# The end of a streaming attention kernel: one store instead of two, and a last weight load cut in two

## The chip, the cores and the metric

The kernel runs on one core of one Trainium2 chip. The metric is the device time of one execution in microseconds, and each kernel was executed several times. The profiled span, from the first to the last instruction of the program, is about 2.1 us shorter than that time: 1321.6 us of span belong to 1323.67 us of time. Times of one kernel scatter by some tenths of a microsecond.

## The reference, cut to what matters

Two decode-attention blocks, A and B, each process a single query row with 32 heads. Their output rows lie side by side.

```python
# A: 32 heads, 32768 cached keys and values of 128 numbers each, one query row of 512 numbers
q = (x @ wq) per head                          # wq: 512 x 4096
p = softmax(q k^T / sqrt(128));  o = p v
a = concat_heads(o) @ wo                       # wo: 4096 x 512 -> one row of 512
# B: the same with 8 shared key/value heads and only the last 4096 keys
out = concatenate([a, b], axis=-1)             # 1 x 1 x 1024, bf16
```

## The kernel before

Almost all the work is streaming the 32 heads of A's caches. This document is about what comes after them: the output projection of A, whose weights `wo` are the last thing that the kernel loads. On the chip `wo` is a tile of 128 partitions, and each partition holds 32 chunks of 512 numbers (1 KB per chunk and partition). Chunk `a` is multiplied by column `a` of the attention output `oz`. The weights come in five loads, cut at these chunks:

```python
WO_CUTS = {"A": (0, 11, 19, 25, 29, 32), "B": (0, 16, 32)}
```

The first eleven chunks accumulate into one full row. All later ones run as pairs: the left and the right half of the row (256 columns each) run side by side on two parts of the matmul array, into rows 0 and 64 of one bank. In the last three pairs of the kernel before, the two halves start 3 to 4 ns apart and the pairs 108 to 109 ns.

```python
def halves(self, e, bank, lhsT, rhs, begin, end, only=(0, 1)):
    for i in only:
        inst = e.matmul(bank[64 * i:64 * i + 1, 0:256], lhsT=lhsT, rhs=rhs[:, 256 * i:256 * i + 256], ...,
                        tile_position=(0, 64 * i))

def store(self, bank, i, dep):
    row = slice(64 * i, 64 * i + 1)
    out, src = self.out_sb[row, :], bank[row, 0:256]
    if i == 0:
        o = self.op("dve", lambda v: v.tensor_copy(out, src), dep)
    else:
        o = self.op("act", lambda e: e.activation(out=out, in_=src, func=ACTF.Copy), dep)
    self.op("act" if i else "sp", lambda e: e.dma_start(self.out[0, :, 256 * i:256 * i + 256], out).then_inc(
        self.outsem[f"A{i}"], 16), o)

def emit_proj(self):
    # ... B's 32 chunks; a copy of their four strips (DVE); `rows`: one f32 matmul that adds them; B's store ...
    # ... chunks 0 to 10 of A into one row; a copy of that row (DVE) ...
    # ... chunks 11 to 30 in pairs, each part waiting for its load; ahead of chunk 25 the row of chunks 0 to 10 is added in ...
    for i in range(2):
        o = self.op("pe", lambda e, i=i: self.halves(e, self.PT, oz[:, 31:32], wo[:, 512 * 31:512 * 32], False, True, (i,)),
                    (self.wosem["A"][-1], 16), self.c["A"]["ozop"])
        self.store(self.PT, i, o)
```

Each half therefore has its own copy engine (the vector engine, DVE, or the scalar engine, ACT), its own store and its own completion semaphore, a counter on which an engine can wait. At the very end the sync engine (SP) waits for the three stores in the order B, A0, A1.

## Time and profile before

| | kernel before |
|---|---|
| time, first 3 runs | 1323.66, 1323.75, 1323.96 us |
| profiled span | 1321.6 us |
| read from HBM | 570.43 MB, 432 GB/s over the span |
| granted TensorE clock | 0.836 of full speed |
| last weights' semaphore full | 1318.848 us |
| end of span minus that | 2.737 us |

The moment at which a load's semaphore is full is called its landing. In the views, PE is the matmul array and PEld its weight loads. Times of single events to a nanosecond, such as the last two rows, come from the semaphore records of the trace, since the views of the profile don't print them. The instruction records show how the sync engine takes its three final waits, in two instructions: a separate event-semaphore instruction (1321.127) waits for A0 and A1, and the branch behind it (1321.204), 77 ns later, carries the wait for B. One view: the chain of work that ended last (start, length, what). These are a few of its pieces from the value matmuls of the last head on:

```profile
1301.34 5.88 PE psACC L656 x64
...
1312.20 0.70 DVE pb L740
1312.91 0.04 issue
1312.95 1.02 PE psACC L741 x2
1313.97 2.27 PE psT L745 x11
1316.24 3.15 PE psPT L719 x42
1319.39 0.02 issue
1319.42 0.41 DVE out_sb L727
```

It names the matmul array, between its stages the vector engine (seven pieces, 2.66 us, of which one is shown), and no load.

### The profile page before, as it was taken

To read this page: it belongs to the slowest core of one execution; us is meant where nothing else is said; L and a number is where in the kernel's file an instruction comes from. 1 tells how busy PE (TensorE), PEld (TensorE's weight loads), DVE (VectorE), ACT (ScalarE), POOL (GpSimd) and SP (SyncE) were. 2 spreads that over 40 slices of the span, in tenths; PEclk is the share of its full clock that TensorE was granted. 3 is DMA by queue.
4 is the path that set the end of the run, shared out by engine and by line. 5 is a ranking of instruction groups with operands and counts; after the bars stand their busy time and mean duration, and the time that the engine had idled before them with its cause. 6 is when DMAs were issued, how large, how long until landed. Compare 5 with 4: busy or idle time off the path is not lost. (4 is left out here: it accounts for less than half of the span.)

```text
span 1321.6 us, 28783 instructions
## 1 busy us (share of the span) xinstructions
PE 969.7 (73%) x13243; PEld 676.6 (51%) x13243; DVE 751.8 (57%) x1341; ACT 55.2 (4%) x168; POOL 2.6 (0%) x22
## 2 busy tenths in 40 slices
PE   4675768777677878776787777678777667877787
PEld 3353446555444655544465544445554445555453
DVE  3563556664555666455566645556665456665564
ACT  0000000000000000000000000000000000000000
POOL 0000000000000000000000000000000000000000
PEclk9886788887878888788888878888887788888788
DMA  9999999999999999999999999999999999999998
GB/s 402 435 436 429 440 432 430 440 434 432 435 434 434 432 436 438 428 436 436 428 438 434 428 438 434 428 440 432 431 440 432 434 434 432 436 432 434 440 428 365
DMA packets 13217, 570.59 MB, mean 432 GB/s; under 512 B 1555, under 2 KB 1558, under 8 KB 1942
## 3 DMA queue, kind: packets, MB, share of 16 engines
q1 hardware_dynamic: 12916, 570.43, 99.8%
q8 instruction: 8, 0.13, 0.0%
q10 hardware_dynamic: 290, 0.00, 0.0%
q14 instruction: 3, 0.02, 0.0%
HBM read 570.43 MB, written 0.00 MB: 432 GB/s over the span
## 5 line engine op out<-in xcount | busy, mean ns | idle before, releaser
L557 DVE COPY kt<-psT 128x1024 bf16<-128x1024 bf16 x1056 | 655.3, 684 | 235.9 <-PE psT L553 234.3
L553 PE MATMUL psT<-ident,kbuf 128*128 128x128 bf16 x8448 | 580.3, 234 | 166.6 <-DMA kbuf<-in_A_k_cache_dram 152.5
L553 PEld LDWEIGHTS psT<-ident,kbuf 128*128 128x128 bf16 x8448 | 540.7, 106 | 258.8 <-DMA kbuf<-in_A_k_cache_dram 160.5
L656 PE MATMUL psACC<-vbuf,ptsb 128*4 128x512 bf16 (+1 forms) x2112 | 187.4, 532 | 22.8 <-ACT ptsb L631 22.0
L576 PE MATMUL psS<-kt,qw 128*32 128x512 bf16 x2048 | 157.7, 385 | 14.8 <-DVE kt L557 14.8
L670 DVE TENSOR_SCALAR oc_A<-psACC,hot_A 128x128 f32<-128x128 f32 x32 | 11.2, 351 | 252.1 <-PE psG L683 252.1
L656 PEld LDWEIGHTS psACC<-vbuf,ptsb 128*4 128x4 bf16 (+1 forms) x2112 | 60.5, 111 | 140.1 <-issue 93.1
L604 ACT ACTIVATE psb<-psS,nb_A 128x512 bf16<-128x512 f32 x32 | 22.0, 687 | 1167.4 <-DVE nb_A L603 1167.4
L576 PEld LDWEIGHTS psS<-kt,qw 128*32 128x32 bf16 x2048 | 34.1, 95 | 57.3 <-DVE kt L557 30.4
L683 PE MATMUL psG<-oc_A,hw 128*32 128x128 f32 (+1 forms) x128 | 19.3, 227 | 52.3 <-DVE oc_A L672 52.3
L683 PEld LDWEIGHTS psG<-oc_A,hw 128*32 128x32 f32 x128 | 11.4, 109 | 62.4 <-DVE oc_A L672 55.0
L628 PE MATMUL psPT<-ident,psb 128*128 128x128 bf16 x136 | 18.2, 278 | 34.0 <-ACT psb L604 34.0
L672 DVE SCALAR_TENSOR_TENSOR oc_A<-psACC,hot_A,oc_A 128x128 f32<-128x128 f32 x96 | 33.7, 351 | 3.4
L593 DVE TENSOR_REDUCE tr_in<-psS 128x1 f32<-128x512 f32 x34 | 23.5, 692 | 17.2 <-PE psS L576 17.2
L628 PEld LDWEIGHTS psPT<-ident,psb 128*128 128x128 bf16 x136 | 10.3, 119 | 37.1 <-ACT psb L604 36.7
L597 PE MATMUL psACC<-rows,tr_in 128*1 128x64 f32 x64 | 8.7, 218 | 25.6 <-DVE tr_in L593 25.6
L631 ACT ACTIVATE ptsb<-psPT 128x512 bf16<-128x512 bf16 x34 | 20.3, 597 | 30.7 <-PE psPT L628 30.7
L597 PEld LDWEIGHTS psACC<-rows,tr_in 128*1 128x1 f32 x64 | 2.7, 81 | 35.1 <-DVE tr_in L593 35.1
L601 PE MATMUL psACC<-mr_A,nscale 1*128 1x1 f32 x64 | 12.1, 256 | 9.8 <-DVE mr_A L600 9.8
L601 PEld LDWEIGHTS psACC<-mr_A,nscale 1*128 1x128 f32 x64 | 9.4, 182 | 15.7 <-DVE mr_A L600 15.7
L495 PE MATMUL psACC<-vbuf,x_B 128*2 128x512 bf16 x32 | 3.6, 625 | 13.7 <-DMA x_B<-in_B_x_dram 13.7
L603 DVE COPY nb_A<-psACC 128x1 f32<-128x1 f32 x32 | 5.0, 158 | 15.0 <-PE psACC L601 15.0
(82 smaller groups left out, 76.5 us busy)
## 6 DMA issues: line engine op xcount, KB each, us to landing
kbuf<-in_A_k_cache_dram SPq DMA_DIRECT2D x4, 4096.0 KB, 23.1
kbuf<-in_B_k_cache_dram SPq DMA_DIRECT2D x2, 4096.0 KB, 31.9
vbuf<-in_B_v_cache_dram SPq DMA_DIRECT2D x2, 4096.0 KB, 25.2
vbuf<-in_B_wq_dram SPq DMA_DIRECT2D x1, 4096.0 KB, 12.7
vbuf<-in_A_wq_dram SPq DMA_DIRECT2D x1, 4096.0 KB, 32.3
kbuf<-in_B_wo_dram SPq DMA_DIRECT2D x2, 2048.0 KB, 33.0
kbuf<-in_A_wo_dram SPq DMA_DIRECT2D x1, 1408.0 KB, 26.1
kbuf<-in_A_wo_dram SPq DMA_DIRECT2D x1, 1024.0 KB, 28.2
```

Of the source, the lines that this page charges most:

```text
L553: inst = e.transpose(T[:, 128 * k:128 * k + 128], src[:, DH * k:DH * k + DH], self.ident[:, :])
L557: self.copies.append(self.op("dve", lambda v: v.tensor_copy(KT[:, :], T[:, :]), o, to="pe"))
L576: inst = e.matmul(self.S[32 * c:32 * c + 32, :], lhsT=win, rhs=self.kt[(bb + c // 2) % NKT][:, 512 * (c % 2):512 * (c % 2) + 512], start=b ...
L593: o = dve(lambda v: v.reduce_max(tr["in"][:, 0:1], self.S[:, :], axis=AXX), self.sdone, self.k_pool, to="pe" if name == "A" else None)
L597: o = self.op("pe", lambda e: e.matmul(self.ACC[0:1, 0:64], lhsT=tr["in"][:, 0:1], rhs=self.rows64[:, :], start=True, stop=True, skip_grou ...
L601: o = self.op("pe", lambda e: e.matmul(self.ACC[:, 64:65], lhsT=self.nscale[:, :], rhs=t["mr"][0:1, :], start=True, stop=True, skip_group_ ...
L604: self.sread = self.op("act", lambda s: s.activation(out=self.psb[:, :], in_=self.S[:, :], func=ACTF.Exp, bias=t["nb"][:, k:k + 1], scale= ...
L628: inst = e.transpose(PT[:, 128 * jj:128 * jj + 128], self.psb[:, 128 * jj:128 * jj + 128], self.ident[:, :])
L631: self.ptread = self.op("act", lambda s: s.activation(out=self.ptsb[:, :], in_=PT[:, 0:512], func=ACTF.Copy), self.psread, to="pe")
L656: inst = e.matmul(acc[32 * c:32 * c + rows, 0:512], lhsT=lhsT, rhs=rhs, start=begin, stop=end, tile_position=(0, 32 * c), skip_group_check ...
L672: o = self.op("dve", lambda v, src=src, hot=hot: v.scalar_tensor_tensor(out=oc, in0=src, scalar=hot, in1=oc, op0=ALU.mult, op1=ALU.add), p ...
L683: return self.op("pe", lambda e: e.matmul(self.G[0:32, c0 + c:c0 + c2], lhsT=win, rhs=t["oc"][g % len(t["oc"])][:, c:c2], start=False, sto ...
```

## The change

Two ideas for the last three microseconds. First, the last load of three chunks becomes one of two and one of a single chunk, so that less work is left when the last bytes arrive. Second, both halves are copied into one row of 512 numbers on one partition, and a single store by the sync engine takes it out.

```diff
-        self.out_sb = sb("out_sb", [128, 256], BF16)
+        self.out_sb = sb("out_sb", [1, 512], BF16)
...
-        self.outsem = {n: s(f"outsem_{n}") for n in ("B", "A0", "A1")}
+        self.outsem = {n: s(f"outsem_{n}") for n in self.X}
...
-    WO_CUTS = {"A": (0, 11, 19, 25, 29, 32), "B": (0, 16, 32)}
+    WO_CUTS = {"A": (0, 11, 19, 25, 29, 31, 32), "B": (0, 16, 32)}
...
     def store(self, bank, i, dep):
-        row = slice(64 * i, 64 * i + 1)
-        out, src = self.out_sb[row, :], bank[row, 0:256]
+        out, src = self.out_sb[0:1, 256 * i:256 * i + 256], bank[64 * i:64 * i + 1, 0:256]
         if i == 0:
-            o = self.op("dve", lambda v: v.tensor_copy(out, src), dep)
-        else:
-            o = self.op("act", lambda e: e.activation(out=out, in_=src, func=ACTF.Copy), dep)
-        self.op("act" if i else "sp", ... one store for each half ...)
+            return self.op("dve", lambda v: v.tensor_copy(out, src), dep)
+        return self.op("act", lambda e: e.activation(out=out, in_=src, func=ACTF.Copy), dep)
...
-            self.store(self.PT, i, o)
+            done.append(self.store(self.PT, i, o))
+        self.op("sp", lambda e: e.dma_start(self.out[0, :, 0:512], self.out_sb[:, :]).then_inc(self.outsem["A"], 16), *done)
```

## The prediction

> **What bounds the kernel now.** I read the page from the top. Transfers come first, in the slices of the span and in the queue table:

> ```profile
> DMA  9999999999999999999999999999999999999998
> ...
> q1 hardware_dynamic: 12916, 570.43, 99.8%
> HBM read 570.43 MB, written 0.00 MB: 432 GB/s over the span
> ```

> The 16 DMA engines are 90% busy or more in every slice but the last, and one load queue fills 99.8% of them. The kernel streams 570 MB at 432 GB/s, and nothing in the change alters a byte of that stream. So about 1318 of the 1321.6 us cannot move. What can move is what comes after the last weights have landed, so I asked for the timeline of the last 3.3 us (start, length, engine, line, [idle before <- who ended it]):

> ```profile
> 1317.80 0.59 PE L719 MATMUL psPT<-pb,e 1*1 1x256 f32 x4
> 1318.33 0.31 PEld L719 LDWEIGHTS psPT<-kbuf,oz_A 128*1 128x1 bf16 x8 [0.44 <-DMA kbuf<-in_A_wo_dram]
> 1318.33 1.06 PE L719 MATMUL psPT<-kbuf,oz_A 128*1 128x256 bf16 x14
> 1318.89 0.20 PEld L719 LDWEIGHTS psPT<-kbuf,oz_A 128*1 128x1 bf16 x6 [0.26 <-DMA kbuf<-in_A_wo_dram]
> 1319.42 0.41 DVE L727 CAST out_sb<-psPT 1x256 bf16<-1x256 f32 x1 [2.36 <-PE psPT L719]
> 1319.45 0.38 ACT L729 ACTIVATE out_sb<-psPT 1x256 bf16<-1x256 f32 x1 [18.04 <-PE psPT L719]
> 1319.86 0.25 SPq L730 DMA_DIRECT2D out_dram<-out_sb  x1
> 1319.86 0.58 ACTq L730 DMA_DIRECT2D out_dram<-out_sb  x1
> ```

> The reader is to see a serial tail: six matmuls that waited for the last load (three chunks, two halves each, from 1318.89), two copies side by side, two stores issued side by side, and then nothing but completion. The waits of the sync engine in that stretch end it:

> ```profile
> SPq L730 <- DVE out_sb L727: 4.8, 1, 4.8
> SPq L437 <- DMA out_dram<-out_sb: 1.0, 1, 1.0
> SPq L101 <- PEq L101: 0.2, 1, 0.2
> ```

> After issuing, the sync engine waits 1.0 us for the stores to complete, then 0.2 us for the other engines. The semaphore records of the trace give the ends that the timeline leaves out: the last weights' semaphore is full at 1318.848; matmul results are announced at 1319.394 (first half) and 1319.428 (second); copies at 1319.840 (DVE) and 1319.835 (ACT); the SP store completes at 1320.927, the ACT store at 1321.111; the sync engine passes at 1321.127 and the span ends at 1321.585.

> [...] both stores start at 1319.86, and the second completes 0.18 us after the first, not with it. [...] no DMA issue here carries two waits, and at the end one such instruction (1321.127) stands before the branch (1321.204), 77 ns apart. [...] Here issue to completion is 1.07 us for 512 B from SP[...].

> **The change part by part.**

> *The load.* The last 3 KB per partition becomes 2 KB and 1 KB; same bytes, one more issue. The sync engine issued the five loads of these weights by 1288.46, some 30 us before they land, so a sixth issue of about 0.43 us is hidden. In the packet records a 4096 B packet takes 159 ns, a 3072 B one 121, a 1024 B one 46: about 38 ns per KB and 7 fixed. Each engine moves 8 rows: eight more packets at 7 ns, less some overlap (3072 B packets follow every 118 ns), plus a 9 ns semaphore packet, is about +0.05 us. The last landing moves from 1318.848 to about 1318.90. The 2 KB load starts, on the slowest engines, where the previous load's semaphore came (last at 1317.948): 8 x 80 ns plus 10 gives 1318.60.

> *The matmuls.* Pairs of halves start every 108 ns (1318.892, 1319.001, 1319.109). Chunks 25 to 28 start at 1318.327, so the array is free at 1318.327 + 4 x 0.108 = 1318.76. It then idles about 0.13 us until the landing, although the view puts the whole 0.26 us of the weight loader down to the DMA. After the change, chunks 29 and 30 run there: 1318.76 to 1318.98. That is satisfied early enough (1318.60), and an already satisfied wait costs no gap: at the boundary of 1316.95 the pairs keep their step. The last chunk can start at max(1318.98, landing 1318.90 + 0.043 reaction) = 1318.98 instead of 1319.109. **Gain: 0.13 us at best; I take 0.12.** It is not the 0.22 us of two pairs, because the array becomes the limit.

> *The copies.* Same two engines, same 256 elements each, about 0.4 us side by side. ACT now writes partition 0 from row 64. I see no reason for another length. Zero.

> *The store.* The ACT store, which completes last, goes: 1321.111 - 1320.927 = 0.184 us. But SP must now wait for both copies. With an event semaphore ahead, the issue comes 77 ns after it, not 16 ns after the copy's semaphore: -0.06 to -0.08. The doubled size adds 46 - 28 = 18 ns by the packet lengths (1024 B and 512 B). **Gain: 0.184 - 0.075 - 0.018 = about 0.09 us.**

> *The end.* Three final waits become two; one event semaphore and one branch should remain. Zero. The smaller row count and larger row of the output buffer shift later SBUF buffers by 512 B; none of them is in the stream. Zero.

> Sum: 0.12 + 0.09 = **0.21 us of 1323.75, or 0.016%**. The time outside the profiled span (1323.67 - 1321.6 = 2.1 us) should not change. Prediction: **1323.5 us**.

> **The rivals.** *The landing takes the gain back*: if 1 KB packets move slower than their fixed part suggests, the last landing comes later than 1318.93 and the last pair waits for DMA again. For it: only one 1 KB packet, a store, stands behind my 46 ns. Against it: 4096 and 3072 B lie on one line with it. It would make 1323.6. *A new wait replaces the old one*: both copies must be ready before any store, and if the event semaphore costs nearer 0.2 us, the store gains nothing. Against it: the copies end within 5 ns of each other, and 77 ns is measured on the same engine. Also 1323.6. *Larger gain*: if the two waits fold into the issue, or chunk 31 is hardly delayed, 0.12 + 0.17 = 0.3 us, so 1323.45; and if one final event-semaphore instruction vanishes, 0.08 more, 1323.4. *Hidden anyway*: the load stream ends a few tenths earlier or later from run to run; the three times before differ by 0.30 us, more than the gain itself. This is the likeliest reason for a result that shows nothing, or a small loss.

> **Range and chances.** The mechanism gives 0 to 0.4 us. The medians of the two kernels each scatter by 0.1 to 0.2, and a different start of the stream may add a few tenths either way. That makes 1323.0 to 1324.0 for 8 in 10. A gain over 2% would need 26 us and a tail of 3.3 us has no such room; a loss of 26 us would need a disturbed load stream, which one extra issue of 128 KB, queued 30 us ahead, does not suggest. Chances: faster 0.005, same 0.99, slower 0.005.

> **What would show it.** In the changed timeline: the pair for chunk 31 starts within 0.15 us of the end of chunk 30, not 0.1 us and more after an idle array; two L719 weight loads, not six, after the last landing; from last landing to the copies' start about 0.40 us (it was 0.57). One store of 1.0 KB from SP, none from ACT, issued some 0.07 to 0.1 us after the copies, completing about 1.1 us later. From the last landing to the end of the span I expect about 2.5 us instead of 2.74. I am wrong about the load if the last pair waits for the landing; about the store if its issue follows the copies at once or comes over 0.15 us later; about the whole if the stream's end moves by more than 0.3 us or its GB/s leaves 432.

## The result, and the profile after

| | before | after |
|---|---|---|
| median of 6 runs each | 1323.96 us (1323.66 to 1324.73) | 1323.63 us (1323.27 to 1324.44) |
| profiled span | 1321.6 us | 1321.3 us |
| last landing | 1318.848 us | 1319.001 us |
| landing to end of span | 2.737 us | 2.333 us |

The ratio is 0.9997, with a 95% interval of 0.9985 to 1.001: the same, at 2%. Ratios here are the mean time of one kernel's fast runs over that of the other's of the same rounds, so not quite the ratio of the quoted medians. The medians differ by 0.33 us, but the two sets overlap over most of their width, so the times alone prove nothing. The profiles can say more, because the tail can be measured piece by piece.

The load stream of the changed kernel, from its queue table, has the same bytes and rate, in 144 more packets (128 rows, whose 3072 B now come as 2048 and 1024 B, and 16 of 4 B, 1282 instead of 1266, as many as the records show raises of the new load's semaphore):

```profile
q1 hardware_dynamic: 13060, 570.43, 99.8%
```

The timeline of its tail:

```profile
1318.15 0.31 PEld L719 LDWEIGHTS psPT<-kbuf,oz_A 128*1 128x1 bf16 x8 [0.44 <-DMA kbuf<-in_A_wo_dram]
1318.71 0.09 PEld L719 LDWEIGHTS psPT<-kbuf,oz_A 128*1 128x1 bf16 x4 [0.25 <-DMA kbuf<-in_A_wo_dram]
1319.04 0.08 PEld L719 LDWEIGHTS psPT<-kbuf,oz_A 128*1 128x1 bf16 x2 [0.25 <-DMA kbuf<-in_A_wo_dram]
1319.35 0.41 DVE L726 CAST out_sb<-psPT 1x256 bf16<-1x256 f32 x1 [3.58 <-PE psPT L719]
1319.39 0.38 ACT L727 ACTIVATE out_sb<-psPT 1x256 bf16<-1x256 f32 x1 [19.33 <-PE psPT L719]
1319.85 0.25 SPq L755 DMA_DIRECT2D out_dram<-out_sb  x1
```

The six weight loads behind the last landing have become four and two. The last two (at 1319.04) still wait for a load, and behind them there is one store. The waits of its sync engine:

```profile
SPq L182 <- ACT out_sb L727: 6.3, 1, 6.3
SPq L101 <- DMA out_dram<-out_sb: 0.8, 1, 0.8
```

Two things are new here. The store's wait for the scalar engine (ACT) is a line of its own, L182, the separate event-semaphore instruction (1319.788), and the issue follows it by 57 ns (1319.845). And the wait for the store's completion (1320.937) has moved from L437 to L101, from such an instruction to the branch behind it (1320.954). The chain that ended last now leads to the load:

```profile
1285.36 31.48 DMA kbuf<-in_A_wo_dram
1316.83 0.04 issue
1316.88 2.45 PE psPT L719 x29
```

Cut at the semaphore records, the tail of the two profiles is:

| piece (us) | before | after | gain |
|---|---|---|---|
| last landing to first matmul result | 0.546 | 0.329 | 0.217 |
| to the last copy's semaphore | 0.446 | 0.447 | 0 |
| to the issue of the last store | 0.016 | 0.068 | -0.052 |
| to the completion of the last store | 1.255 | 1.092 | 0.163 |
| to the end of the span | 0.474 | 0.397 | 0.077 |
| sum | 2.737 | 2.333 | 0.404 |

The span fell by only 0.25 us, since the last landing itself came 0.153 us later in this profile.

### The profile page after: what moved, and what is told of

Its sections match the earlier page's. It is cut to its first block, busy times and chain, and to the rows that moved or that the text cites. A ratio compares the mean times of both kernels' runs of the same rounds, so it can differ in the third digit from the quotient of the medians.

```text
span 1321.3 us, 28784 instructions
## 1 busy us (share of the span) xinstructions
PE 967.9 (73%) x13243; PEld 675.8 (51%) x13243; DVE 752.0 (57%) x1341; ACT 55.2 (4%) x168; POOL 2.6 (0%) x22
## 2 busy tenths in 40 slices
DMA  9999999999999999999999999999999999999998
## 3 DMA queue, kind: packets, MB, share of 16 engines
q1 hardware_dynamic: 13060, 570.43, 99.8%
HBM read 570.43 MB, written 0.00 MB: 432 GB/s over the span
## 5 line engine op out<-in xcount | busy, mean ns | idle before, releaser
L656 PE MATMUL psACC<-vbuf,ptsb 128*4 128x512 bf16 (+1 forms) x2112 | 183.9, 524 | 22.8 <-ACT ptsb L631 22.0
```

Source lines behind the costliest of these rows:

```text
L656: inst = e.matmul(acc[32 * c:32 * c + rows, 0:512], lhsT=lhsT, rhs=rhs, start=begin, stop=end, tile_position=(0, 32 * c), skip_group_check ...
```

## The experiments

The theory to test is that the tail is a fixed sum of these pieces behind a load stream that jitters. The rivals are that the tail itself is noise, that one part does everything, and, as the prediction had it, that the matmul array and not the landing is what the last pair waits for. A single execution has no others beside it that would tell whether it ran undisturbed (its state is "unknown" in the record), so of such runs only the pieces of the profiles are used. (The times of the first four, before_again, store_only, split_only and after_end_swapped, were 1323.53, 1323.59, 1323.28 and 1324.02 us beside 1323.67 us for the kernel before. Those of before_end_swapped, store_from_act and six_last were 1323.76, 1324.08 and 1324.19 us beside a median of 1323.64 us. They differ more by where the landing and the chain of section 8 fell than by the edits.)

### 1. The kernel before, once more

No edit.

> The kernel before, unchanged, for a second profile. Theory (a fixed tail behind a jittering load stream): from the last weights' landing to the end of the span 2.74 us again within 0.05, made of 0.546 to the matmul result, 0.446 copies, 1.27 to the ACT store's completion, 0.474 to the end; the landing itself may move by some tenths of a us. Rival (the 0.25 us between the two profiled spans is only noise of the tail): landing to end moves by 0.2 us or more between two profiles of the same kernel.

Measured: 2.738 us from landing to end, in the pieces 0.547, 0.447, 0.017, 1.254 and 0.473. No piece moved by more than 1 ns, while the landing moved by 0.179 us (1318.669). The tail is no noise. Over all profiles the least steady piece, the completion of the store, spreads by 7 ns with two stores and by 11 ns with one store from the sync engine, so a difference of some 20 ns can be read from a single profile.

### 2. The store alone

```diff
 (changed kernel)
-    WO_CUTS = {"A": (0, 11, 19, 25, 29, 31, 32), ...}
+    WO_CUTS = {"A": (0, 11, 19, 25, 29, 32), ...}
```

> One store by the sync engine, but the last load still of three chunks. Theory: landing to end 2.74 - 0.11 (store) - 0.077 (end) = 2.55 us, with 0.546 us from landing to matmul result as before. Rival (the split does all the work, the store is given back to the new wait): 2.74 us. Rival (the store does all): 2.33 us.

Measured: 2.554 us, in the pieces 0.546, 0.446, 0.069, 1.096 and 0.397. The store gives 0.107 us and the end 0.077.

### 3. The split alone

```diff
 (kernel before)
-    WO_CUTS = {"A": (0, 11, 19, 25, 29, 32), ...}
+    WO_CUTS = {"A": (0, 11, 19, 25, 29, 31, 32), ...}
```

> The last load split into two and one chunks, but two stores as before. Theory: landing to matmul result 0.33 us instead of 0.546 (two pairs of 108 ns fewer), store and end as before, so landing to end 2.74 - 0.217 = 2.52 us; from the previous load's semaphore (29 chunks landed) to the last landing 0.94 us instead of 0.90. Rival (the matmuls are hidden behind the landing or the array is the limit): landing to result falls by 0.13 us or less. Rival (1 KB packets are slow): last landing comes 0.1 us or more later after the semaphore of the 29 chunks.

Measured: 2.526 us, in the pieces 0.329, 0.447, 0.017, 1.259 and 0.474. Its timeline shows both halves of the argument, the shorter array work and the unchanged pair of stores:

```profile
1318.37 0.09 PEld L719 LDWEIGHTS psPT<-kbuf,oz_A 128*1 128x1 bf16 x4 [0.26 <-DMA kbuf<-in_A_wo_dram]
1318.70 0.08 PEld L719 LDWEIGHTS psPT<-kbuf,oz_A 128*1 128x1 bf16 x2 [0.25 <-DMA kbuf<-in_A_wo_dram]
...
1319.45 0.58 ACTq L730 DMA_DIRECT2D out_dram<-out_sb  x1
1319.45 0.25 SPq L730 DMA_DIRECT2D out_dram<-out_sb  x1
```

From the semaphore of the load that ends with chunk 28 to the last landing it took 0.930 us. Over all profiles with the old cuts at 29 and 32 this distance is 0.897 to 0.911 us, mean 0.90, and over the eight with the cuts at 29, 31 and 32 it is 0.925 to 0.982, mean 0.945. The price of the extra load is thus about 0.045 us, and the split is worth 0.217 - 0.045 = 0.17 us where the landing decides.

### 4. and 5. The order of the final waits

The prediction expected nothing from the end; the profile showed 0.077 us. The two runs change only the order in which the sync engine waits for the stores, once in each kernel.

```diff
 (changed kernel)
-        for n in self.outsem:              # A, B
+        for n in ("B", "A"):
             self.op("sp", lambda e, n=n: e.wait_ge(self.outsem[n], 16))
 (kernel before)
-        for n in self.outsem:              # B, A0, A1
+        for n in ("A1", "B", "A0"):
```

> The changed kernel, with the two final waits in the other order, so that the store that completes last is waited for by the separate event-semaphore instruction and not by the branch. Theory (the end got shorter because the last wait sits on the branch): completion to end of span 0.47 us instead of 0.397, so landing to end 2.41 instead of 2.33. Rival (the end got shorter because the scalar engine has no store, or because there is one semaphore less): 0.397 us, unchanged.

> The kernel before, with the final waits ordered so that the scalar engine's store, which completes last, is waited for by the branch. Theory (place of the last wait): completion to end 0.397 us instead of 0.474, with both stores kept; landing to end 2.66 us. Rival (it needs one store): 0.474 us, unchanged.

Measured from completion to end: 0.453 us in the changed kernel (0.397 without the swap), 0.397 us in the kernel before (0.474). The waits of the swapped changed kernel name L437 again, where the changed kernel had L101:

```profile
SPq L437 <- DMA out_dram<-out_sb: 0.8, 1, 0.8
```

The theory holds in both directions, and the rival, that it needs a single store, falls. The first wait written ended up on the branch; the others went into an event-semaphore instruction ahead of it (1321.127 and 1320.145 in the two kernels' profiles). Where the store that completes last was waited for there, the branch followed late: by 0.077 us with two waits in that instruction, by 0.056 us with one. The kernel before could have had these 0.077 us with both of its stores.

The swapped changed kernel did not show the expected 2.41 us from landing to end but 3.009, because its last pair started 0.6 us late. This was the first sign of the second chain; see 8.

### 6. The one store, issued by the scalar engine

```diff
-        self.op("sp", lambda e: e.dma_start(self.out[0, :, 0:512], ...
+        self.op("act", lambda e: e.dma_start(self.out[0, :, 0:512], ...
```

> The changed kernel, its one store issued by the scalar engine instead of the sync engine. Theory[...]: issue about 0.33 us long or less, and about 1.1 us from issue to completion, as from the sync engine. Rival (the scalar engine's issue is slow by itself): about 0.58 us long and 1.25 us to completion.

The timeline has the issue:

```profile
1320.44 0.51 ACTq L755 DMA_DIRECT2D out_dram<-out_sb  x1
```

Neither side was right as a whole. Alone, the scalar engine's issue takes 0.508 us, not 0.33, the 0.583 us of the kernel before less the 0.249 us of the sync engine's issue: it is slow by itself, and beside the sync engine's issue it was only 0.075 us longer (0.583). But from issue to completion it takes 1.126 us, close to the 1.092 us of the sync engine and far from 1.255. So of the 0.184 us that the scalar engine's store came later in the kernel before, about 0.13 (1.255 - 1.126, for 512 B and 1 KB; by the packet lengths the size is worth some 0.02 more) belongs to two stores issued at once. The runs don't show what about the second issue costs it.

### 7. One semaphore for both copies

Both copies count up the same semaphore, and the store waits once, for two.

```diff
-            return self.op("dve", lambda v: v.tensor_copy(out, src), dep)
+            self.op("dve", lambda v: v.tensor_copy(out, src).then_inc(self.osem, 1), dep)
 ... the same for the scalar engine's copy ...
-        self.op("sp", lambda e: e.dma_start(...).then_inc(self.outsem["A"], 16), *done)
+        self.op("sp", lambda e: e.dma_start(...).then_inc(self.outsem["A"], 16), (self.osem, 2))
```

> The changed kernel, both copies counting up one semaphore, so that the store carries a single wait for two. Theory (the separate event-semaphore instruction ahead of the store costs 0.05 us): last copy to issue 0.016 us instead of 0.068, landing to end 2.28 us instead of 2.33; the time shows nothing, since three times of one kernel differ by 0.3 us and more. Rival (the 0.068 us is the sync engine's own decoding or the copies' release): 0.068 us, unchanged.

Measured: 0.020 us from the last copy to the issue instead of 0.068, so the separate instruction cost 0.048 us, and a wait that counts two copies avoids it. The rival falls. The median of four runs was 1323.44 us (1323.38 to 1324.47), that of seven of the kernel before on the same chip 1323.64 (1323.57 to 1324.14); ratio 0.9997, 0.9981 to 1.0014. The profile fell on the slowest of the four executions, and its last pair was 1.23 us late, so from landing to end it took 3.524 us for the 2.28 expected. Its tail shows why:

```profile
1318.95 0.09 PEld L720 LDWEIGHTS psPT<-pb,e 1*1 1x1 f32 x4 [0.22 <-issue]
...
1319.47 0.63 PEld L720 LDWEIGHTS psPT<-kbuf,oz_A 128*1 128x1 bf16 x14 [0.44 <-issue]
...
1320.88 0.25 SPq L756 DMA_DIRECT2D out_dram<-out_sb  x1
```

All fourteen weight loads form one group without any wait for a load: by 1319.47 the last chunk (landed at 1318.852) was long there, and the array was simply not done with earlier work.

### 8. A last load of six chunks

```diff
-    WO_CUTS = {"A": (0, 11, 19, 25, 29, 31, 32), ...}
+    WO_CUTS = {"A": (0, 11, 19, 23, 26, 32), ...}
```

> The changed kernel, its last two loads of three and six chunks instead of two and one. Theory (each pair of matmuls after the last landing costs 108 ns, as nothing hides it): landing to matmul result 0.33 + 5 x 0.108 = 0.87 us, landing to end 2.87 us, with store and end as in the changed kernel. Rival (the array catches up, its pairs run at another pace or overlap the landing): below 0.7 us.

Measured: 1.243 us from landing to the result, 3.251 to the end. The run missed its aim: the price of a pair cannot be read from it, since its array too was late. Four of the first eight runs were in this state, so it needed a theory of its own. From the first value matmul of the last head (the first product of its softmax weights with its cached values) to the last pair's start those four took 17.70 to 17.72 us. From this the theory: **the last pair starts at the later of two times**, the last landing plus 0.046 us (plus 0.108 us for each further pair of the last load), or the first value matmul of the last head plus 17.69 us.

| profile | first value matmul | by the load | by the array | last pair, measured |
|---|---|---|---|---|
| before | 1301.344 | 1319.110 | 1319.034 | 1319.112 |
| before_again | 1301.127 | 1318.931 | 1318.817 | 1318.932 |
| before_end_swapped | 1301.555 | 1319.271 | 1319.245 | 1319.273 |
| store_only | 1299.973 | 1319.210 | 1317.663 | 1319.212 |
| split_only | 1300.012 | 1318.708 | 1317.702 | 1318.710 |
| after | 1299.988 | 1319.047 | 1317.678 | 1319.048 |
| after_end_swapped | 1301.874 | 1318.962 | 1319.564 | 1319.584 |
| store_from_act | 1301.936 | 1319.050 | 1319.626 | 1319.635 |
| one_sem | 1302.414 | 1318.898 | 1320.104 | 1320.132 |
| six_last | 1302.109 | 1319.432 | 1319.799 | 1319.806 |

The two numbers were fitted to these ten, so the agreement to 28 ns proves little yet. Nor is the chain quite fixed: up to the start of chunk 25 it took 16.99 to 17.02 us in the three profiles of the kernel before and 17.04 to 17.07 in the four late ones. The next runs test it.

### 9. The array's chain made longer

```diff
+        def twice(e):
+            for _ in range(2):
+                inst = e.matmul(self.ACC[0:1, :], lhsT=self.e32[:, 0:1], rhs=self.pb[:, :], start=True, stop=True, ...)
+            return inst
-        rows = o = self.op("pe", lambda e: e.matmul(self.ACC[0:1, :], ...), strips, self.accread)
+        rows = o = self.op("pe", twice, strips, self.accread)
```

> The changed kernel with the one-row gather of the other output (two passes, 0.86 us on the matmul array) done twice, so that the array's work after the last head is 0.86 us longer and nothing else differs. Theory (the last pair starts at the later of two ends: 0.046 us after the last landing, or a fixed array chain after the first value matmul of the last head, 17.69 us until now): the array's end becomes 17.69 + 0.86 = 18.55 us after that matmul, and the later of the two is the measured start, within 0.05 us. Rival (the late ends of four runs came from the semaphore or the landing of the last load and not from the array): the last pair follows the landing by 0.05 us, or is late by an amount that the 18.55 us do not give.

The first value matmul came at 1302.045, so 1320.595 was expected for the last pair; measured 1320.599, against a landing at 1318.860. The two lines of its timeline that matter are the doubled matmul and the last, unbroken group:

```profile
1313.71 1.88 PE L739 MATMUL psACC<-pb,e 128*1 128x512 f32 x4 [0.80 <-DVE pb L736]
...
1319.94 0.93 PE L719 MATMUL psPT<-kbuf,oz_A 128*1 128x256 bf16 x14
```

Its time was 1324.98 us. The array's chain does set the end when it is the later one, and no load or semaphore needs to be blamed.

### 10. and 11. The array's chain made shorter

The [0.80 <-DVE pb] in that line is time in which the array stands idle, waiting for a copy of B's strips. The first eleven chunks of A don't need that copy, so they can go ahead of it. Run 10 does this in the changed kernel with one semaphore for both copies (7), run 11 in the kernel before.

```diff
-        rows = o = self.op("pe", ... one-row gather of B ..., strips, self.accread)
-        ... its copy and B's store ...
         row = self.proj_part("A", 0, ...)        # chunks 0 to 10
+        rows = o = self.op("pe", ... one-row gather of B ..., strips, self.accread)
+        ... its copy and B's store ...
```

> The changed kernel with one semaphore for both copies, and with the first eleven weight chunks multiplied ahead of the one-row gather of the other output instead of behind it, so that the array does not stand idle for the copy that the gather waits for (0.80 us). Theory: the array chain is 17.69 - 0.80 = 16.89 us from the first value matmul of the last head; the last pair starts at the later of that and of the landing plus 0.046 us; from landing to end 2.28 us where the landing is later. In time a gain of 0.3 to 0.6 us over the kernel before in the runs where the array would have been late, less elsewhere; three decimals below 2%, so the verdict is the same. Rival (the gather or its copy is delayed in turn, or eleven chunks wait for their load): the chain stays at 17.69 us.

> The kernel before with that reordering alone. Theory: array chain 16.89 us, last pair 0.26 us after the landing (three pairs), landing to end 2.74 us as before wherever the landing is later than the array; the time at or a few tenths of a us below the kernel before. Rival (the array chain plays no part in the kernel before): same as before in every run, and the chain still 17.69 us.

The timeline of run 10:

```profile
1312.24 2.54 PE L739 MATMUL psT<-kbuf,oz_A 128*1 128x512 bf16 x11
1312.34 0.69 DVE L738 COPY pb<-psS 128x512 f32<-128x512 f32 x1 [1.65 <-PE psS L735]
...
1318.77 0.08 PEld L720 LDWEIGHTS psPT<-kbuf,oz_A 128*1 128x1 bf16 x2 [0.24 <-DMA kbuf<-in_A_wo_dram]
```

The copy now runs beside the eleven matmuls. In this profile the first value matmul came at 1301.424; with the old chain the array would have held the last pair until 1319.114, and it started at 1318.772, 0.048 us after the landing. So the chain is at least 0.34 us shorter; the full 0.80 was not seen, as the landing came later. Up to the start of chunk 25 it is 0.54 to 0.62 us shorter (16.44 us against the 16.99 to 17.07 above). A little of the rival came true as well: the eleven chunks started 0.05 us after their own load had landed (1312.193), about 0.12 us later than the array could have begun at its pace. Landing to end: 2.283 us (2.28 expected), and 2.746 us in run 11 (2.74 expected). The profile of run 11 says nothing of the chain, since its first value matmul came at 1299.762 and even the old chain would have ended 1.5 us before the last pair; only its times bear on that.

Times, on one chip and in the same rounds:

| kernel | runs (us) | median |
|---|---|---|
| before | 1323.49, 1323.50, 1323.61, 1323.65, 1323.84, 1324.08, 1324.51, 1324.60, 1324.79 | 1323.84 |
| before_array_early | 1323.45, 1323.48, 1323.55, 1323.55, 1323.75 | 1323.55 |
| after_again | 1323.11, 1323.28, 1323.32, 1323.79, 1324.38 | 1323.32 |
| array_early | 1322.98, 1323.10, 1323.10, 1323.14, 1323.43 | 1323.10 |

All four are the same at 2% (ratios to before 0.9997, 0.9997 and 0.9994, each interval including 1). Still, all five times of array_early lie below all nine of the kernel before, and it beats both kernels of this study in the median. Under the kernel before it lies by 0.74 us, more than the 0.3 to 0.6 expected, with few runs behind it. And the slow tail of the times is missing from the two reordered kernels: 7 of the 23 runs of the kernel before in all sets were above 1324.0 us, 3 of 11 of the changed kernel (six and five runs), but none of these 10.

### 12. The changed kernel, once more

> The changed kernel, unchanged, again with times. Theory: last pair at the later of landing plus 0.046 us and of 17.69 us after the first value matmul of the last head; from the last pair's start to the end of the span 2.29 us in either case (the kernel before: 2.47 us). Its times scatter by 0.5 us and more, as the array's chain falls behind the landing in some runs and not in others; the median 0.0 to 0.4 us under the kernel before. Rival (one fixed gain of 0.25 us as between the first two spans): each time about 0.25 us below the kernel before, no more scatter than that one's.

Measured: landing 1318.895, by the load 1318.941, by the array 1317.648, last pair 1318.944, landing to end 2.331 us, last pair to end 2.282 us (2.29 expected). The five times are in the table above: four at 1323.11 to 1323.79 and one at 1324.38. They don't separate theory and rival: they spread over 1.27 us, those of the kernel before in the same rounds over 1.30 us. What speaks against one fixed gain are the profiles of sections 8 and 9, not these times.

### Where the array's chain gets its delay

The first value matmul came at 1299.8 to 1300.0 us in five of the fourteen profiles and at 1301.1 to 1302.4 in nine. The mean granted clock between 1260 and 1280 us splits them without exception. The windows of the kernel before, of the changed kernel and of one_sem (start:end, length, busy time of five engines, granted clock, DMA share, GB/s):

```profile
1260.00:1280.00 20.00, 14.11 (x164) 8.41 (x162) 7.50 (x16) 1.59 (x5) 0.00 (x0) 0.74 1.05 452
```

```profile
1260.00:1280.00 20.00, 14.12 (x205) 8.76 (x202) 9.57 (x20) 1.58 (x5) 0.00 (x0) 0.91 1.04 449
```

```profile
1260.00:1280.00 20.00, 14.09 (x155) 8.04 (x153) 7.15 (x15) 1.59 (x5) 0.00 (x0) 0.74 1.04 447
```

## Why the prediction was right or wrong

Predicted were 1323.5 us and "same"; measured were 1323.63 us and "same". The bound was read correctly: the stream sets the time (its queue fills 99.8% in both profiles), and the change moved only tenths of a microsecond behind it. Step by step:

- **The load: right.** Predicted was a landing 0.05 us later; measured a mean distance from the landing of the first 29 chunks of 0.945 instead of 0.90 us. Its own sign of an error here ("if the last pair waits for the landing") did come, but because the array was early, not because the landing was late.
- **The matmuls: one term wrong.** The step "It is not the 0.22 us of two pairs, because the array becomes the limit" failed. In the changed kernel's profile the array was free early, the last pair followed the landing by 0.047 us, and the piece shrank by the whole 0.217 us; net of the later landing that is 0.17 us and not 0.12. The idea of a competing array was right, but the prediction froze one draw of it. (A small slip beside it: from 1318.76 the array idles 0.13 us until the next pair starts at 1318.892, and 0.09 us until the landing.) The array's end was only 0.03 to 0.11 us ahead of the load's in the three profiles of the kernel before without reordering, 1.0 to 1.6 us ahead in store_only, split_only and both profiles of the changed kernel, and up to 1.2 us behind in others. (This is by the fitted 17.69 us; counted from the start of chunk 25 at 108 ns a pair, the first three are 0.05 to 0.15 us ahead.)
- **The copies: right**, 0.446 and 0.447 us.
- **The store: right in sum, 0.11 us for 0.09.** The event semaphore ahead of the issue came as the prediction had it, and cost 0.052 us for the predicted 0.06 to 0.08. The doubled size cost about 0.02 us (1.092 after 1.071) for 0.018. What was misread, in the expectation of section 6, is the length of ACT's issue: at most 0.075 of its 0.583 us goes with the other issue, as ACT alone takes 0.508. It did not enter the sum.
- **The end: wrong.** "One event semaphore and one branch should remain. Zero." They do remain, but the new order puts the last completion on the branch: 0.077 us. The rival "Larger gain" held this 0.08 as a possibility, for another reason (the instruction vanishing).
- **The whole.** Landing to end was expected at 2.5 us and is 2.33. The gain is 0.404 - 0.045 = 0.36 us in executions where the landing is later. Where the array is later, the split buys nothing by the same sum and only 0.19 us are left, for store and end. The medians (0.33 and 0.52 us lower in two sets of rounds) lie around that, inside their scatter. The prediction's 0.21 us was too small by the pair and the end, and that the time came out close is luck: the scatter is larger than either error, and the kernel before itself rose from 1323.75 us (three runs) to 1323.96 (six), which more than made up for a gain larger than forecast. The rival "Hidden anyway", that the start of the tail moves by a few tenths from run to run, was right about the times; but in the profiles the larger part of that movement is the array's chain and not, as it said, the load stream: the last landing lay within 0.37 us in all fourteen, and the chain, where no edit lengthened it, made the last pair up to 1.23 us late.

## What to carry to other kernels

When a kernel streams at its limit, look for every chain that ends near the last landing: here the last pair started at the later of two, and the chain that lost by 0.03 us in one profile won by 1.2 us in another. A single tail is best compared piece by piece between semaphores, where one profile repeated to some ten nanoseconds here, while five to nine runs of the whole time did not settle a gain of 0.3 us. Small waits have a place as well as a length: let one semaphore count several producers (0.048 us here), and put the wait that is satisfied last on the last instruction (0.056 to 0.077 us here).
